# Last three chunk passes: second feed-forward product by seven block products for eight, with a copy of x for the norms

## The chip, the core and the metric

The kernel runs on one core of one Trainium2 chip (trn2). The core's engines have queues of their own: PE (matrix products, with PEld for loading the stationary operand), DVE (elementwise work and reductions), ACT (scaled copies, exponentials, SiLU), POOL (here: memsets and the starting of some DMAs) and SP (here: it only starts DMAs). The instructions of one engine run in the order in which they were written for it, and wait for other engines by semaphores. The metric is device time in microseconds (us).

## The reference

Two layers over 2048 tokens of width 576, each made of a sliding attention and a feed-forward part. In float32:

```
x = x + attention(layernorm(x), wqkv) @ wo
x = x + silu(layernorm(x) @ w1) @ w2          # w1: 576 x 4608, w2: 4608 x 576
x = x + attention(layernorm(x), wqkv) @ wo    # the same weights again
x = x + silu(layernorm(x) @ w1) @ w2
```

Attention has 32 heads of 18 columns; every token looks at itself and at the seven tokens 2, 4, ... 14 before it.

## The kernel before

**Passes.** The tokens are worked in chunks of 512 (NJ = 4 tiles of 128). With two layers this makes eight passes, s = 0 to 7; passes 4 to 7 are the second layer. `front(s)` holds the attention of pass s (norm, query-key-value product in four column units u, attention arithmetic, output projection, norm for the feed-forward part), and `ffn` or `ffn_pairs` its feed-forward part. The attention of pass s+1 runs beside the feed-forward part of pass s.

**Numbers.** Every float32 operand of a product is held as two float16 halves, high and low, and a product takes three float16 products (high by high, high by low, low by high).

**Feed-forward from pass 2 on (`ffn_pairs`).** The 36 row blocks of w1 and w2 are taken as 18 pairs, six groups (g) of three pairs. The first product of a pair is already done by seven block products P1 to P7 for eight (line 1096, 7 matmuls each, from weight forms that were made ahead and lie in DRAM as `wfs`). ACT copies partial results out of PSUM (L1100), DVE adds others (L1103), ACT applies SiLU (L1119, L1121, L1123), ACT makes the high half (L1126) and DVE the low half (L1129, one instruction over 1024 columns). The second product (`second`, L1151) takes 48 matmuls of 128x288 for a pair: 4 token tiles x 2 row blocks x 3 half products x 2 column halves. After each token tile of a group DVE adds the PSUM sum to x (`add_to`, L861). So the second product of a group stands behind the first products of its three pairs, and PE fills the time with first products of the next group. Two PSUM areas (`acc`) take turns for the second product, four banks (z, misc) for the first.

**Attention on DVE.** For one column unit: two products q by k over 2304 columns (L782) with a reduction each (L786), the softmax pieces, four products of weights by v over 1152 columns (L815), and two trees of additions (L822, L823). POOL starts the four small copies between partitions for the halo (L763). The query-key-value product is L682, the projection L854.

**Order.** All work is recorded as operations with an engine, an estimated length, what they read and write, and a priority (`prio`, mostly s plus a fraction; smaller goes first). `Plan.order` plays a list schedule over these estimates and writes the instructions in the order in which they start in it. Buffers are areas of SBUF that several names share; an operation waits until a slot of its name is free.

Of the kernel before, what the change touches and what calls it, by code (L numbers as in the profile page):

```python
# [264 lines left out]
def sliding_attention_silu_ffn(ctx: ExitStack, tc: tile.TileContext, x, wqkv, wo, w1, w2, out):  # L265
# [10 lines left out]


# [50 lines left out]
    part("yb", XA, 1, [8, KH], F32, turns=False)  # L328
# [15 lines left out]
    parts("yf", [(YH, 0), (YO, 0)], [2, KB], F16)  # L344
# [6 lines left out]
    part("w2", W2A, W2N, [2, D], F16)  # L351
# [20 lines left out]
    wfs = [tc.dram_tile([P, 7 * KB], F16, name=f"wfs{q}") for q in range(NP)]  # L372
    wqs = [tc.dram_tile([P, 30 * UC], F16, name=f"wqs{u}") for u in range(NU)]
# [42 lines left out]
    dz = accw[:, NP:NP + NP // 2, :].rearrange("p a b -> p (a b)")  # L416
    pace = cp.tile([1, 1], F32, name="pace")
# [57 lines left out]
    highs = []  # L475
    turned = []
# [21 lines left out]
    def layer_norm(xs, prio, into, on_act, on_pe=False, late=[]):  # L498
# [77 lines left out]
    def raw_wq(u):  # L576
# [3 lines left out]
        raw = lambda k: fl(T(rs[k]).bitcast(F32))[:, :QR]  # L580
# [132 lines left out]
    def attention(s, xT, wq, more=None):  # L713
# [4 lines left out]
        for u in range(NU):  # L718
            kv, qt = Buf("kv"), Buf("qt")
            own = [(kv, j) for j in range(NJ)]  # L720
            if wq is None:
# [8 lines left out]
            else:  # L730
                w = wq(u)
                if blk == 0:
# [3 lines left out]
                    op("POOL", 1.86, clear, [], [(kv, "edge")], pr_)  # L736
                else:
# [5 lines left out]
                    op("SP", 0.8, edge, [("eds", lay, par, u)], [(kv, "edge")], pr_, nbytes=20000, lanes=2)  # L743
                for j in range(NJ):
# [31 lines left out]
            keys = own + [(kv, "halo"), (kv, "edge")]  # L776
            lg, pe, mx, sm = Buf("lg"), Buf("pe"), Buf("mx"), Buf("mx")
            for j in range(0, NJ, 2):
# [9 lines left out]
                op("DVE", 2.49, mul, keys + [(qt, j), (qt, j + 1)], [pr], pr_)  # L788
                op("DVE", 2.49, red, [pr], [(lg, j)], pr_)
# [8 lines left out]
            def soft_b(pe=pe, sm=sm):  # L798
# [5 lines left out]
            op("DVE", 1.42 if blk == 0 else 0.98, soft_a, [], lgs + [mx], pr_)  # L804
            op("ACT", 0.36, lambda pe=pe, lg=lg: nc.scalar.activation(T(pe), T(lg), AF.Exp, scale=DH ** -0.5),
               lgs, [pe], pr_ - 0.2, table="exp")
            op("DVE", 1.38, soft_b, [], [pe, sm], pr_)
            for j in range(0, NJ, 2):
                pr = Buf("pr")

                for a in range(2):
# [5 lines left out]
                    op("DVE", 1.28, mul, keys + [pe], [(pr, a)], pr_, after=formed[-1:])  # L817
# [6 lines left out]
                op("DVE", 2.55, tree, [], [(pr, 0), (pr, 1), (o, j, u), (o, j + 1, u)], pr_, after=formed[-1:])  # L824
                if s == 0:
                    marks.append(op("POOL", 1.3, lambda j=j, u=u: nc.gpsimd.tensor_copy(
                        pace, T(o)[0:1, j, u * UC:u * UC + 1]), [(o, j, u)], ["pace"], -5))
# [69 lines left out]
    def raw_split(f0, prio):  # L897
# [440 lines left out]
```

## Time and profile before

| what | value |
|---|---|
| three timed runs | 2138.58, 2142.57, 2148.47 us (median 2142.57) |
| span of the profiled execution, first to last instruction | 2139.6 us |
| busy, whole span | PE 2114.5, DVE 1640.1, ACT 977.0, POOL 365.9 us |
| read from DRAM, written | 307.32 MB, 67.68 MB |
| DMA engines, mean rate | 199 GB/s |

The profile records no total of its own for the profiled execution beside the span; the span lies 1.0 us above the fastest of the timed runs and 3.0 us under their median. Busy time of PE counts each matmul from start to a modelled end, and neighbouring matmuls overlap, so the rate of PE is read from starts, not from the mean length of one.

### The profile page before, as it was taken

To read this page: it belongs to the slowest core of one execution; us is meant where nothing else is said; L and a number is where in the kernel's file an instruction comes from. 1 tells how busy PE (TensorE), PEld (TensorE's weight loads), DVE (VectorE), ACT (ScalarE), POOL (GpSimd) and SP (SyncE) were. 2 spreads that over 40 slices of the span, in tenths; PEclk is the share of its full clock that TensorE was granted. 3 is DMA by queue.
4 is the path that set the end of the run, shared out by engine and by line. 5 is a ranking of instruction groups with operands and counts; after the bars stand their busy time and mean duration, and the time that the engine had idled before them with its cause. 6 is when DMAs were issued, how large, how long until landed. Compare 5 with 4: busy or idle time off the path is not lost.

```text
span 2139.6 us, 41351 instructions
## 1 busy us (share of the span) xinstructions
PE 2114.5 (99%) x16233; PEld 1576.2 (74%) x16233; DVE 1640.1 (77%) x2599; ACT 977.0 (46%) x1803; POOL 365.9 (17%) x585
## 2 busy tenths in 40 slices
PE   8999899999999999999999999999999999999999
PEld 5556466656667888877788777887788877888887
DVE  8999999999977997548975599746997569853322
ACT  7555787644254553344424344343443434333332
POOL 2223656234242430001100010000000000000000
PEclk9999999999999999999999999999999999999999
DMA  6576777677799987775748765596565965566551
GB/s 182 154 228 245 250 262 247 197 266 237 197 234 287 325 248 209 175 214 167 211 121 224 201 180 160 138 248 190 157 175 146 250 178 165 162 156 199 152 169 62
DMA packets 334235, 426.21 MB, mean 199 GB/s; under 512 B 145608, under 2 KB 262708, under 8 KB 330072
## 3 DMA queue, kind: packets, MB, share of 16 engines
q1 hardware_dynamic: 293720, 293.19, 49.5%
q0 software_dynamic: 38304, 129.28, 18.8%
q8 instruction: 127, 2.08, 0.4%
q10 hardware_dynamic: 2016, 1.11, 0.2%
q14 instruction: 68, 0.56, 0.1%
HBM read 307.32 MB, written 67.68 MB: 175 GB/s over the span
## 4 chain that ended last, share of the span: by engine, by line
PE 88%; DMA 6%; DVE 3%; issue 1%; ACT 1%; SPq 1%; POOL 0%; ACTq 0%; DVEq 0%; POOLq 0%
PE acc L1151 28%; PE z L1096 13%; PE misc L1096 13%; PE z L1193 9%; PE acc L1212 9%; PE z L682 7%; PE acc L854 5%; PE misc L682 5%; DMA w<-wfs 1%; DMA xb<-yo 1%; DMA h<-in_A_wqkv_dram 1%; DMA w<-in_B_w_dram 1%; DMA w<-w2s 1%; DMA yo<-yh 0%; DMA x<-xd 0%
## 5 line engine op out<-in xcount | busy, mean ns | idle before, releaser
L1151 PE MATMUL acc<-w,h 128*128 128x288 f16 x5184 | 669.0, 286 | 1.6 <-DVE x L861 1.0
L1151 PEld LDWEIGHTS <-h 128*128 128x128 f16 x5184 | 507.2, 98 | 126.8 <-issue 2.2
L1096 PEld LDWEIGHTS <-w 128*128 128x128 f16 x5292 | 517.3, 98 | 72.0 <-DMA w<-wfs 3.7
L1096 PE MATMUL z<-xb,w 128*128 128x256 f16 x2653 | 335.5, 273 | 2.3 <-DMA w<-wfs 1.7
L1096 PE MATMUL misc<-xb,w 128*128 128x256 f16 x2639 | 335.7, 273 | 1.1 <-DVE hs L1103 0.9
L861 DVE SCALAR_TENSOR_TENSOR x<-acc,d,x 128x576 f32<-128x576 f32 x183 | 148.5, 812 | 129.8 <-PE acc L1151 122.2
L1212 PE MATMUL acc<-w,h 128*128 128x288 f16 x1728 | 215.4, 286 | 0.0
L682 PEld LDWEIGHTS <-xa 128*128 128x128 f16 x1344 | 131.0, 98 | 112.9 <-issue 2.1
L1212 PEld LDWEIGHTS <-h 128*128 128x128 f16 x1728 | 168.4, 98 | 44.2
L782 DVE TENSOR_TENSOR prs<-qt,kvs 128x2304 f32<-128x2304 f32 x64 | 163.4, 2552 | 10.3 <-DMA kvs<-kvs 9.4
L815 DVE TENSOR_TENSOR prs<-kvs,pe 128x1152 f32<-128x1152 f32 x128 | 170.8, 1351 | 0.5
L786 DVE TENSOR_REDUCE lg<-prs 128x128 f32<-128x2304 f32 x64 | 163.0, 2547 | 1.0
L822 DVE TENSOR_TENSOR prs<-prs 128x1152 f32<-128x1152 f32 (+1 forms) x128 | 135.1, 1055 | 3.1
L1129 DVE SCALAR_TENSOR_TENSOR h<-wq,sh,h 128x1024 f16<-128x1024 f32 x60 | 76.8, 1280 | 73.3 <-ACT h L1126 73.3
L1193 PE MATMUL z<-xb,w 128*128 128x512 f16 x588 | 129.1, 379 | 3.3 <-ACT w L931 1.6
L682 PE MATMUL z<-wq,xa 128*128 128x432 f16 x658 | 124.4, 346 | 0.0
L854 PE MATMUL acc<-wo,yo 128*128 128x288 f16 x896 | 114.2, 286 | 3.7 <-DMA yo<-yh 2.0
L1100 ACT ACTIVATE wq<-z 128x256 f32<-128x256 f32 x94 | 35.6, 381 | 171.4 <-PE z L1096 171.4
L1193 PEld LDWEIGHTS <-w 128*128 128x128 f16 x588 | 57.3, 98 | 72.0 <-DVE w L933 2.9
L854 PEld LDWEIGHTS <-yo 128*128 128x128 f16 x896 | 87.3, 98 | 27.9 <-DMA yo<-yh 2.8
L763 POOL DMA_DIRECT2D kvs<-kvs x64 | 34.0, 538 | 419.1 <-ACT qt L751 418.9
L682 PE MATMUL misc<-wq,xa 128*128 128x432 f16 x518 | 99.1, 346 | 2.7 <-ACT xa L463 1.3
(229 smaller groups left out, 2578.7 us busy)
## 6 DMA issues: line engine op xcount, KB each, us to landing
w<-wfs SPq DMA_DIRECT2D x756, 160.0 KB, 3.4
w<-w2s SPq DMA_DIRECT2D x252, 288.0 KB, 4.4
wq<-wqs SPq DMA_DIRECT2D x17, 1080.0 KB, 6.2
kvs<-kd POOLq DMA_DIRECT2D x8, 1584.0 KB, 9.2
w<-w1s SPq DMA_DIRECT2D x36, 320.0 KB, 4.3
wfs<-xa POOLq DMA_DIRECT2D x18, 640.0 KB, 4.9
w2s<-w POOLq DMA_DIRECT2D x36, 288.0 KB, 4.1
w1s<-wq POOLq DMA_DIRECT2D x30, 320.0 KB, 4.0
```

Source lines behind the costliest of these rows:

```text
L682: nc.tensor.matmul(T(m)[:, :3 * UC], a, b, start=n == 0, stop=n == len(pl) - 1)
L782: nc.vector.tensor_tensor(T(pr), T(qt)[:, j:j + 2, None, :].to_broadcast([P, 2, W, UC]), win(T(kv), j, 2), op=ALU.mult)
L786: nc.vector.tensor_reduce(T(lg)[:, j:j + 2].rearrange("p a w h -> p (a w h)"), T(pr).rearrange("p a w (h d) -> p (a w h) d", d=DH), axis=A ...
L815: nc.vector.tensor_tensor(T(pr)[:, a].rearrange("p w (h d) -> p w h d", d=DH), v, T(pe)[:, j + a, :, :, None].to_broadcast([P, W, UH, DH]) ...
L822: nc.vector.tensor_tensor(t[:, :, 0:h, :], t[:, :, 0:h, :], t[:, :, h:2 * h, :], op=ALU.add)
L854: nc.tensor.matmul(T(acc)[:, h, 0:288], a, b[:, h * 288:(h + 1) * 288], start=n == 0, stop=n == len(pl) - 1)
L861: nc.vector.scalar_tensor_tensor(t, T(acc)[:, :, 0:288], d, t, op0=ALU.mult, op1=ALU.add)
L1096: nc.tensor.matmul(t, w[:, u, :], v[:, r, :], start=first and m == 0, stop=m == 6, skip_group_check=True)
L1129: op("DVE", 1.2, lambda hq=hq, h=h, sc=sc: nc.vector.scalar_tensor_tensor(T(h)[:, 1].rearrange("p f t -> p (f t)"), T(hq).rearrange("p r t ...
L1151: nc.tensor.matmul(T(acc)[:, h, 0:288], T(hb[t])[:, a, f, j * P:(j + 1) * P], T(wbs[t][f])[:, w, h * 288:(h + 1) * 288], start=t == 0 and ...
L1193: nc.tensor.matmul(T(z), v, u, start=m == 0, stop=m == len(pl) - 1)
L1212: nc.tensor.matmul(T(acc)[:, h, 0:288], T(hb[q])[:, a, j * P:(j + 1) * P], T(wbs[q][0])[:, w, h * 288:(h + 1) * 288], start=q == 0 and m = ...
```

## The change

In passes 5, 6 and 7 the second product is done in blocks too (`ffn_twice`, `seconds`): tokens in two halves, columns in two halves, the two row blocks of a pair as the third dimension; seven block products (`SECOND`) take the place of eight. Each is 18 matmuls of 128x288 for a group of three pairs. For this the activations of a pair are kept as seven rows of 256 tokens in place of four: POOL makes four of them by subtractions and one addition (L1268), the high and low halves are made in two pieces (rows 0 to 2 over 768 columns, rows 3 to 6 over 1024; L1273 on ACT, L1276 on DVE). A group has seven additions to x (L1316) in place of four.

Of the seven weight blocks three are column halves of w2 as stored (the store order becomes column half, then high and low), and four are sums. `prepare_second` makes these once per pair and stores them as `wts`: pairs 0 to 8 after the attention arithmetic of pass 4, pairs 9 to 17 after that of pass 5. It uses the area of the key-value buffers, so the query-key-value products of units 0 and 1 of passes 5 and 6 wait for the last store of these forms (`hold`).

In the second layer the norm ahead of the attention reads a copy of x that is loaded a second time, into the area of the attention products (`xp` in `prs`), after the attention arithmetic of the pass before. x itself lies in tiles of two token blocks. Priorities: DVE work of the attention of passes 6 and 7 gets a later one (`pd`, with LEAD), and the second products of a pass's last group get pp + SEAM. Some estimated lengths change. Pass 7 has buffers of its own for more slots (`q2e`, `wte`).

```diff
+S3 = 5
+LEAD = 0.05
+SEAM = 1.0
...
+    part("xp", PR, 1, [NJ, D], F32)
...
-    part("w2", W2A, W2N, [2, D], F16)
+    part("w2", W2A, W2N, [2, 2, KH], F16)
...
+    parts("h2", [(HA, 0), (HA, FB), (HA, 2 * FB), (W2A, 0), (W2A, FB)], [2, 7, 2 * P], F16)
+    parts("q2", [(WQA, 20 * 3 * UC), (W2A, 2 * FB)], [7, 2 * P], F32)
+    parts("wt", [(HA, 3 * FB + i * WB) for i in range(4)] + [(W2A, 3 * FB + i * WB) for i in range(3)]
+          + [(WQA, 20 * 3 * UC + FB)], [2, KH], F16)
+    parts("q2e", [(WQA, 0), (WQA, 20 * 3 * UC), (W2A, 2 * FB)], [7, 2 * P], F32)
+    parts("wte", [(t, i * WB) for t in (PR, O, XA) for i in range(8)], [2, KH], F16)
+    parts("v2", [(KV, 0), (KV, 10 * WB)], [20 * KH], F16)
...
+                hold = {S3: [("wts", NP // 2 - 1)], S3 + 1: [("wts", NP - 1)]}.get(s, []) if u < 2 else []
...
+            pd = pr_ if s <= S3 else pr_ - 0.5 + 0.1 * u + LEAD
...
+    def prepare_second(q, prio, after):
...
+        def sums():
+            t = rows6()
+            for r, x, y in ((3, 1, 0), (1, 5, 1), (4, 5, 3), (2, 2, 4)):
+                nc.gpsimd.tensor_tensor(t[:, r], t[:, x], t[:, y], op=ALU.subtract)
+        op("POOL", 3.4, sums, [(b, 0)], [(b, 0)], prio)
+        op("ACT", 1.2, lambda: nc.scalar.activation(split()[:, :, 0, :], rows6()[:, 1:5], AF.Copy, scale=wst[:, q:q + 1]),
+           [(b, 0), "wsc"], [(b, 1)], prio)
+        op("DVE", 1.4, lambda: nc.vector.scalar_tensor_tensor(split()[:, :, 1, :], rows6()[:, 1:5], wst[:, q:q + 1], split()[:, :, 0, :],
+                                                              op0=ALU.mult, op1=ALU.subtract), [(b, 0), (b, 1)], [(b, 1)], prio)
+        op("POOL", 0.57, lambda: nc.gpsimd.dma_start(wts[q], T(b)[:, 12 * KH:]), [(b, 1)], [("wts", q)], prio, nbytes=P * 4 * KH * 4)
...
+    SECOND = (1, 5, 6, 3, 7, 2, 4)
+    def ffn_twice(s, xf, xs):
...
+                for r, u, v, o in ((4, 6, 3, ALU.add), (5, 4, 0, ALU.subtract), (2, 1, 5, ALU.subtract), (6, 0, 6, ALU.subtract)):
+                    op("POOL", 0.75, lambda hq=hq, r=r, u=u, v=v, o=o: nc.gpsimd.tensor_tensor(T(hq)[:, r], T(hq)[:, u], T(hq)[:, v], op=o),
+                       [(hq, u), (hq, v)], [(hq, r)], pd - 0.01)
+                for r0, r1, sh in ((0, 3, shx), (3, 7, shy)):
...
+    def seconds(s, g, q0, n, hb, xs):
...
+        wb = {(k, t): load_wt(q0 + t, k, s - 0.5, "wt" if s < NL * NC - 1 else "wte") for k in SECOND for t in range(n)}
+        for i, k in enumerate(SECOND):
...
+                        for j in js:
+                            for t in ts:
+                                for m, (a, w) in enumerate(((0, 0), (0, 1), (1, 0))):
+                                    nc.tensor.matmul(T(acc)[:, j, 0:KH], T(hb[t])[:, a, row[k], j * P:(j + 1) * P], T(wb[k, t])[:, w, :],
...
-            o = attention(s, layer_norm(X[s], s - 1.0, "xa", False, late=[("wfs", NP - 1, 1)]), lambda u: load_wq(u, s - 1.0, "wz"))
+            o = attention(s, layer_norm(load_x(s, s - 1.0, attended[-1:], into="xp"), s - 1.0, "xa", False, late=[("wfs", NP - 1, 1)]), lambda u: load_wq(u, s - 1.0, "wz"))
...
-        (ffn if s < S2 else ffn_pairs)(s, XT[s], X[s])
+        (ffn if s < S2 else ffn_pairs if s < S3 else ffn_twice)(s, XT[s], X[s])
...
+        if s in (S3 - 2, S3 - 1):
+            for q in range(*((0, NP // 2), (NP // 2, NP))[s - S3 + 2]):
+                prepare_second(q, s + 0.9, attended[s + 1:s + 2])
```

How the instructions then stand is shown at three places. The first is DVE in the third group of pass 5, between additions to x, where the attention of pass 6 (L815, L822, L823 before; L813, L854 of the changed file, the same operations) runs beside the feed-forward part. Before:

```order
L861 SCALAR_TENSOR_TENSOR x_80<-acc_104,d_270,x_80 128x576
L1129 SCALAR_TENSOR_TENSOR h<-wq,sh_267,h 128x1024
L815 TENSOR_TENSOR prs<-kvs,pe_87 128x1152
L822 TENSOR_TENSOR prs<-prs 128x2x576
L822 TENSOR_TENSOR prs<-prs 128x2x288
L823 TENSOR_TENSOR o<-prs 128x2x144
L861 SCALAR_TENSOR_TENSOR x_81<-acc_105,d_270,x_81 128x576
```

And of the change, at the same group (L1316 is the addition to x, L1244 an addition of a first product, L1276 one half of the low halves):

```order
L854 TENSOR_TENSOR o<-prs 128x2x144
L1316 SCALAR_TENSOR_TENSOR x_76<-acc_99,d2x,x_76 128x2x288
L1244 TENSOR_TENSOR wq<-z_95,wq 128x256
L1244 TENSOR_TENSOR wq<-misc_96,wq 128x256
L1276 SCALAR_TENSOR_TENSOR w_87<-w_87,shx 128x768
L1316 SCALAR_TENSOR_TENSOR x_75<-acc_98,d2x,x_75 128x2x288
L1276 SCALAR_TENSOR_TENSOR w_87<-w_87,shy 128x1024
L813 TENSOR_TENSOR prs<-qts,kvs 128x2304
```

The additions to x stand closer together (seven to a group), and the low halves are two instructions, so more feed-forward work lies between two pieces of attention.

The second place is POOL beside the feed-forward part of pass 6, near its last halo copies. Before, POOL starts the four halo copies of a unit and then DMAs of x to the output, and nothing else:

```order
L763 DMA kvs<-kvs 112x1152
L763 DMA kvs<-kvs 15x1152
L763 DMA kvs<-kvs 112x864
L763 DMA kvs<-kvs 14x864
L1234 DMA out_dram<-x_78 128x576
```

With the change (L1268 is the arithmetic on the activations, L793 the halo):

```order
L1268 TENSOR_TENSOR wq<-wq 128x256 x4
L1268 TENSOR_TENSOR w_87<-w_87 128x256 x3
L793 DMA kvs<-kvs 112x1152
L793 DMA kvs<-kvs 15x1152
L793 DMA kvs<-kvs 112x864
L793 DMA kvs<-kvs 14x864
L1268 TENSOR_TENSOR w_87<-w_87 128x256
```

Four instructions of arithmetic for every pair stand in POOL's queue between the halo copies, and here a pair's last one stands behind a halo.

The third place is ACT in pass 7, one pair. Before (L1100 copies out of PSUM, L1121, L1123 and L1119 are SiLU, L1126 the high half; the last row is the next pair's):

```order
L1100 ACTIVATE wq<-z_100 128x256
L1100 ACTIVATE wq<-z_101 128x256 x2
L1121 ACTIVATE wq<-wq,accw 128x512
L1123 ACTIVATE wq<-wq,accw 128x256
L1119 ACTIVATE wq<-z_101,accw 128x256
L1126 ACTIVATE h<-wq,sh_267 128x1024
L1100 ACTIVATE wq<-misc_103 128x256
```

With the change (L1241 copies out of PSUM, L1262, L1264 and L1260 are SiLU, the two L1273 the high halves; tiles `w_87` are this pair's, `wq` the next one's):

```order
L1241 ACTIVATE w_87<-z_94 128x256
L1241 ACTIVATE w_87<-misc_96 128x256 x2
L1262 ACTIVATE w_87<-w_87,accw 128x2x256
L1264 ACTIVATE w_87<-w_87,accw 128x256
L1260 ACTIVATE w_87<-misc_96,accw 128x256
L1241 ACTIVATE wq<-z_95 128x256
L1273 ACTIVATE h<-w_87,shy 128x1024
L1273 ACTIVATE h<-w_87,shx 128x768
L1241 ACTIVATE wq<-misc_97 128x256
```

Between SiLU and the high halves now lies POOL's arithmetic, and a copy out of PSUM for the next pair stands behind the high halves on ACT.

More of the change, by code (lines that the diff above doesn't have):

```diff
@@ L372, in sliding_attention_silu_ffn @@
     wfs = [tc.dram_tile([P, 7 * KB], F16, name=f"wfs{q}") for q in range(NP)]
+    wts = [tc.dram_tile([P, 4 * 2 * KH], F16, name=f"wts{q}") for q in range(NP)]
     wqs = [tc.dram_tile([P, 30 * UC], F16, name=f"wqs{u}") for u in range(NU)]
@@ L534, in layer_norm @@
                 prio = -19
-            y, yh = Buf("y"), Buf("yh")
+            own = xs[j][0].tag == "xp"
+            y, yh = xs[j] if own else Buf("y"), Buf("yq" if own else "yh")
             def norm(j=j, y=y):
@@ L720, in attention @@
             own = [(kv, j) for j in range(NJ)]
+            free = formed[-1:] if u == 1 and s > NC else ()
             if wq is None:
@@ L735, in clear @@
                         nc.gpsimd.memset(T(kv)[0:1, 3:7], 0.0)
-                    op("POOL", 1.86, clear, [], [(kv, "edge")], pr_)
+                    op("POOL", 1.86, clear, hold, [(kv, "edge")], pr_, after=free)
                 else:
@@ L753, in attention @@
                         op("PE", 2.56 * (b - a) / 14, lambda j=j, m=m, w=w, a=a, b=b: qkv_matmul(xT, w, j, m, a, b),
-                           [(xT, j)] + [w.keys[5 * h + k] for k in range(a // 3, (b + 2) // 3) for h in range(2)],
-                           [m, (kv, "hold")] if lay else [m], pr_)
+                           [(xT, j)] + hold + [w.keys[5 * h + k] for k in range(a // 3, (b + 2) // 3) for h in range(2)],
+                           [m, (kv, "hold")] if lay else [m], pr_, after=free)
                     op("ACT", 0.78, evac, [m, ("su", u)], [(kv, j), (qt, j)], pr_ - (0 if s else 9))
@@ L823, in tree @@
                     nc.vector.tensor_tensor(T(o)[:, j:j + 2, u * UC:(u + 1) * UC], t[:, :, 0, :], t[:, :, 1, :], op=ALU.add)
-                op("DVE", 2.55, tree, [], [(pr, 0), (pr, 1), (o, j, u), (o, j + 1, u)], pr_, after=formed[-1:])
+                done = op("DVE", 2.55, tree, [], [(pr, 0), (pr, 1), (o, j, u), (o, j + 1, u)], pd, after=formed[-1:])
                 if s == 0:
@@ L827, in attention @@
                         pace, T(o)[0:1, j, u * UC:u * UC + 1]), [(o, j, u)], ["pace"], -5))
+        attended.append(done)
         return o
@@ L832, in project @@
         pr_ = s - 1.0
+        pd = pr_ if s <= S3 else pr_ - 0.5 + 0.4 + LEAD
         for j in range(NJ):
@@ L1031, in sliding_attention_silu_ffn, with forms @@
     P_ORDER = ("P5", "P1", "P3", "P6", "P2", "P7", "P4")
-    def forms(xs, prio, home="yb", late=[]):
+    def forms(xs, prio, home="yb"):
         st, mv, nt = Buf("st"), Buf("mv"), Buf("nt")
@@ L1242, in write_x, with load_x @@
                     op("SP", 0.5, lambda j=j, c0=c0: nc.sync.dma_start(x_rows(out, c, j)[:, c0], T(xs[j])[:, c0]),
-                       [(xs[j], h)], [], pd, nbytes=P * D * 2)
-    def load_x(s, prio, ahead=None):
-        lay, c = divmod(s, NC)
-        xs = [Buf("x") for _ in range(NJ)]
+                       [(*xs[j], h)], [], pd, nbytes=P * D * 2)
+        if s == NL * NC - 1 and S3 < NL * NC:
+            for th, ch in ((0, 1), (0, 0), (1, 1), (1, 0)):
+                for i in range(2):
+                    j, c0 = 2 * th + i, slice(ch * KH, (ch + 1) * KH)
+                    op("SP", 0.38, lambda j=j, c0=c0: nc.sync.dma_start(x_rows(out, c, j)[:, c0], T(xs[j])[:, c0]),
+                       [(*xs[j], ch)], [], pd, nbytes=P * D * 2)
+    def load_x(s, prio, ahead=None, into=None):
+        lay, c = divmod(s, NC)
+        if into is None:
+            halves = [Buf("x") for _ in range(2)]
+            xs = [(halves[j // 2], j % 2) for j in range(NJ)]
+        else:
+            b = Buf(into)
+            xs = [(b, j) for j in range(NJ)]
         for j in range(NJ):
             src = (lambda j=j: x_rows(x, c, j)) if lay == 0 else (lambda j=j: xd[c][j])
-            if ahead:
+            if ahead and lay == 0:
                 op("POOL", 0.54, lambda j=j, src=src: nc.gpsimd.dma_start(T(xs[j]), src()), [], [xs[j]], prio,
```

221 lines of the change are left out of this document (171 added, 50 removed).

## The prediction

> **What bounds the kernel now.** I read the page first: its span, the busy shares and the 40 slices.
>
> ```profile
> span 2139.6 us, 41351 instructions
> ...
> PE 2114.5 (99%) x16233; PEld 1576.2 (74%) x16233; DVE 1640.1 (77%) x2599; ACT 977.0 (46%) x1803; POOL 365.9 (17%) x585
> ...
> PE   8999899999999999999999999999999999999999
> ...
> DVE  8999999999977997548975599746997569853322
> ...
> POOL 2223656234242430001100010000000000000000
> ```
>
> PE is busy in every slice, POOL nearly idle in the second half, and DVE reaches 9 in places there. Busy matmuls overlap, so I checked the rate of PE in order of time, in the first full group of pass 7, and two pieces of the chain that ended last, of the attention (start us, length us):
>
> ```profile
> 1957.50 6.04 PE L1151 MATMUL acc<-w,h 128*128 128x288 f16 x48
> 1963.38 0.93 PE L1096 MATMUL z<-xb,w 128*128 128x256 f16 x7
> 1964.15 0.93 PE L1096 MATMUL misc<-xb,w 128*128 128x256 f16 x7
> ```
>
> ```profile
> 1485.15 5.11 PE misc L682 x28
> ...
> 1614.82 3.43 PE acc L854 x28
> ```
>
> 48 matmuls of 128x288 take from 1957.50 to 1963.38, that is 0.1225 us each; seven of 128x256 take 0.765 us, 0.1093 each; L682 takes 5.11/28 = 0.1825, L854 0.1225. A group of pass 7 has 147 and 144 matmuls of the first two kinds: 16.07 + 17.64 = 33.71 us. The table by stage has it at 33.69, and shows the stretches that hold most of passes 5 and 6 (columns: length, then busy time of PE, PEld, DVE, ACT, POOL, clock, DMA share, GB/s):
>
> ```profile
> 1957.67:1991.36 33.69, 33.69 (x293) 28.49 (x292) 10.58 (x16) 11.79 (x21) 0.00 (x0) 1.00 0.52 156
> ```
>
> ```profile
> 450.00:700.00 250.00, 248.03 (x1666) 162.70 (x1664) 221.15 (x314) 112.11 (x175) 83.61 (x123) 1.00 0.89 257
> ...
> 1410.00:1660.00 250.00, 249.88 (x2024) 197.91 (x2023) 186.98 (x290) 97.33 (x191) 10.70 (x20) 1.00 0.67 185
> 1660.00:1910.00 250.00, 250.00 (x2021) 197.50 (x2020) 187.46 (x290) 97.40 (x194) 10.69 (x20) 1.00 0.65 180
> ```
>
> So passes 5 to 7 are PE's own work with no gap, at full granted clock; a matmul removed there is time saved, as long as nobody else becomes late. DVE has 63 us to spare in 250.
>
> **What the change removes.** For each pair 48 matmuls of the second product become 42. Three passes of 18 pairs: 54 x 6 = 324 matmuls fewer; 324 x 0.1225 = **39.7 us**. Each still loads its own stationary operand, as before.
>
> **What it adds on DVE.** The rows by form, of the last 730 us:
>
> ```profile
> L861 DVE SCALAR_TENSOR_TENSOR x<-acc,d,x 128x576 f32<-128x576 f32 x74 | 60.3, 814 | 87.5 <-PE acc L1151 87.4
> L1129 DVE SCALAR_TENSOR_TENSOR h<-wq,sh,h 128x1024 f16<-128x1024 f32 x36 | 46.1, 1281 | 58.5 <-ACT h L1126 58.5
> L815 DVE TENSOR_TENSOR prs<-kvs,pe 128x1152 f32<-128x1152 f32 x32 | 42.8, 1351 | 0.1
> L782 DVE TENSOR_TENSOR prs<-qt,kvs 128x2304 f32<-128x2304 f32 x16 | 40.9, 2556 | 6.2 <-DMA kvs<-kvs 5.8
> L786 DVE TENSOR_REDUCE lg<-prs 128x128 f32<-128x2304 f32 x16 | 40.8, 2551 | 0.4
> L1103 DVE TENSOR_TENSOR wq<-z,wq 128x256 f32<-128x256 f32 x58 | 23.8, 419 | 25.8 <-ACT wq L1100 20.4 <-PE z L1096 5.3
> ...
> L822 DVE TENSOR_TENSOR prs<-prs 128x1152 f32<-128x1152 f32 x16 | 21.6, 1352 | 0.2
> ...
> L822 DVE TENSOR_TENSOR prs<-prs 128x576 f32<-128x576 f32 x16 | 12.1, 758 | 0.6
> L823 DVE TENSOR_TENSOR o<-prs 128x288 f32<-128x288 f32 x16 | 7.3, 458 | 0.6
> ```
>
> The split of 768 columns is new; between the 576 columns of L861 (0.81) and the 1024 of L1129 (1.28) I take 1.0. A pass then has 18 x 1.0 more for the splits and 18 more additions to x at 0.81 (42 for 24), 33 us together: 187 + 33 = 220 of the some 240 us that passes 5 and 6 keep. That fits as an average, but not everywhere. The attention of pass 6 cannot begin until the weight forms are stored, so it is pressed into a part of pass 5. I counted the order of the change there, from the first block product of the second group to the third of the fifth, 23 block products, on both queues. PE: 476 of 128x256, 414 + 112 of 128x288, 112 of L682: 52.0 + 50.7 + 13.7 + 20.4 = 137 us. DVE, 213 instructions: attention arithmetic 81 us (6 of L782, 6 of L786, 16 of L815, 8 trees at 2.57, softmax 8), splits of nine pairs 20.6, 28 additions of first products 11.8, 23 additions to x 18.7, norms and projection about 27: 159 us by mean lengths. Instructions that do not use the one before start earlier:
>
> ```profile
> 1583.28 0.42 DVE L1103 TENSOR_TENSOR hs<-z,hs 128x256 f32<-128x256 f32 x1
> 1583.62 0.41 DVE L1103 TENSOR_TENSOR hs<-misc,hs 128x256 f32<-128x256 f32 x1
> ```
>
> 0.34 us apart at a length of 0.42; with 0.08 off for some 90 of the 213, DVE needs 152. That is 15 more than PE's 137, and PE cannot run away from it: the block product after the next needs the PSUM area that DVE's addition empties. An addition may lag by one block product (18 x 0.1225 = 2.2 us) and a little more, so 12 to 15 are lost; I take **12**, and 0 to 15 as bounds, 0 if work between is overlapped better than counted. The same count over the first four groups of pass 6 gives PE 161, DVE 151: 10 us of slack. In pass 7 DVE has no attention beside it and waits.
>
> **What it adds on POOL.** Four instructions of 256 columns for a pair, reading two tiles in SBUF. The trace has no such instruction. Nearest rows:
>
> ```profile
> L734 POOL MEMSET kvs<- 2x864 f32 x12 | 9.7, 810 | 120.7 <-DVE prs L815 120.7
> ...
> masks.py:199 POOL TENSOR_SCALAR_AFFINE_SELECT ident<-ident 128x128 f16<-128x128 f16 x1 | 0.3, 289 | 0.1
> ```
>
> Between 0.29 (half the columns) and 0.81 (over three times as many, none read); I take 0.6, twice the first. A chain of four is then 2.4 us in a pair's 10.5. POOL has room. But one kind of POOL instruction in the trace reads SBUF, a copy of a single element, and its length depends on DVE:
>
> ```profile
> 82.53 2.56 POOL L826 COPY pace<-o 1x1 f32<-1x1 f32 x1 [1.44 <-DVE o L823]
> ...
> 132.90 0.18 POOL L826 COPY pace<-o 1x1 f32<-1x1 f32 x1 [17.84 <-DVE o L823]
> ```
>
> ```profile
> 82.48 2.56 DVE L782 TENSOR_TENSOR prs<-qt,kvs 128x2304 f32<-128x2304 f32 x1
> ...
> 132.96 1.55 DVE L668 SCALAR_TENSOR_TENSOR wo<-w,su,wo 128x576 f16<-128x576 f32 x2 [0.19 <-ACT wo L665]
> ```
>
> Begun 0.05 us after an L782 of DVE, which reads two tiles, it ends with that, 2.56 us later; with DVE idle at its start it takes 0.18. So POOL's arithmetic will wait for DVE. Whether DVE also waits for POOL the trace cannot show, since a one-element copy is over at once. Bounds for DVE's wait per POOL instruction: 0, and 0.6, its whole length. I take 0.2, a third, because only part of DVE's instructions read two tiles in SBUF, and some begin when POOL is nearly done. In the overfull stretch of pass 5 are nine pairs, 36 such instructions: **8 us**. In pass 6, 48 x 0.2 = 10 meets the slack of 10: 0. [...]
>
> **What I cost at nothing.** The weight forms: on POOL, ACT and DVE a few us for each of 18 pairs, in groups around the change of pass, where by the same count DVE has 24 to 28 us of work beside 54 to 56 of PE; the queue of PE holds the query-key-value product behind the last of them, and if that is late, PE waits: at most some 6 us, twice. ACT: two high halves for one, 17 us more a pass on 97 busy in 250. DMA, all on SP's queue: seven loads of 144 KB a pair for two of 288, and x again, some 9 MB a pass, 185 to about 227 GB/s. The window 450 to 700 above ran 257 GB/s with PE busy 248 of 250, so that is the cover.
>
> ```profile
> w<-wfs SPq DMA_DIRECT2D x756, 160.0 KB, 3.4
> w<-w2s SPq DMA_DIRECT2D x252, 288.0 KB, 4.4
> ```
>
> Passes 5 and 6 hold eight block weights, and a block product uses three in 2.2 us, so a freed place has about 3.7 us when products stand back to back, and a landing takes 3.4 to 4.4. First products mostly stand between; without them it costs up to 1 us each, some 20 in all.
>
> **The sum.** 2139.6 - 39.7 + 12 + 8 = 2119.9 for the profiled execution. Its span lies 3.0 under the median of the runs, so I say **2123 us** against 2142.57, 0.9% faster. Likeliest case, 2114 to 2132: 0.45.
>
> **Rivals.**
> - *Everything is hidden*: DVE's excess is taken up by lag and POOL does not hold DVE. 2142.6 - 39.7 = 2103, up to 2114. For it: no DVE instruction in the trace was held; against: the count of 152 to 137. Chance 0.18.
> - *POOL and DVE shut each other out*, slower. If each POOL instruction keeps DVE for its 0.6 us, pass 5 loses 12 + 36 x 0.6 = 34, pass 6 48 x 0.6 - 10 = 19, and the later halves make ACT and PE wait besides: 2142.6 - 39.7 + 53 = 2156 and more, up to 2175. It is even with the gain at 39.7 = 12 + 84t - 10, t = 0.45 us. [...] Chance 0.15.
> - *Gain given back in small waits*: port 0.3 to 0.45 us, block weights late by 5 to 15, forms late by 5. 2132 to 2153. Chance 0.22.
> - *The change does not do what it says*: the order has 324 matmuls fewer on PE, in the passes named. I leave nothing for it.
>
> **How the numbers follow.** The range goes from the bottom, 2103, to 2153; it leaves out the slow rival at 0.15 and a little below. A measurement of this kernel can tell about 0.5%, 10.7 us, from no change: faster is under 2132 (0.45 + 0.18), same 2132 to 2153 (0.22), slower above (0.15).
>
> **What would show it.** Groups of pass 7 at 147 x 0.1093 + 126 x 0.1225 = 31.5 us: the 39.7 is right. PE waits of 15 to 25 us between the second and the fifth group of pass 5, released by DVE, and hardly any in pass 6: my terms. [...] PE waiting for ACT L1273 or for block weights in passes 6 and 7 would make me wrong, as would a wait at the start of the query-key-value product of pass 5 or 6.

## The result, and the profile after

The changed kernel takes 2192.41 us, median of four runs (2187.96 to 2198.82), beside 2140.57 us for the kernel before (2137.69 to 2148.47): ratio 1.0239, interval 1.0217 to 1.0261. It is 2.4% slower; 2123, a little faster, was forecast. The profiled execution has a span of 2186.2 us, 46.6 more than before.

The page of the change, parts 1 and 2 (busy time of each engine; the span in 40 slices):

```profile
span 2186.2 us, 42078 instructions
...
PE 2096.9 (96%) x15909; PEld 1548.1 (71%) x15909; DVE 1794.8 (82%) x2729; ACT 1038.2 (47%) x1875; POOL 645.2 (30%) x891
...
PE   8999899999999999999999999989889899998999
...
DVE  8999999999978999699943799856999699974454
...
POOL 2223665233233230110222111352332234222222
```

PE has 324 matmuls fewer, and for the first time slices under 9 in the second half. DVE stands at 9 in longer stretches, POOL has work to the end. Two windows of 250 us, which were full before, and two groups of pass 7 (columns as in the prediction: length, busy time of PE, PEld, DVE, ACT, POOL, clock, DMA share, GB/s):

```profile
1410.00:1660.00 250.00, 222.26 (x1709) 168.69 (x1707) 201.40 (x242) 106.33 (x195) 92.12 (x96) 0.97 0.73 204
1660.00:1910.00 250.00, 230.04 (x1814) 177.16 (x1812) 221.16 (x309) 106.27 (x201) 81.45 (x84) 0.99 0.74 203
2043.80:2077.50 33.70, 33.70 (x296) 28.67 (x294) 16.36 (x25) 15.12 (x27) 8.55 (x12) 1.00 0.72 209
2077.50:2106.70 29.20, 29.20 (x254) 24.69 (x253) 14.79 (x22) 12.55 (x21) 8.59 (x12) 1.00 0.73 209
```

In pass 7, with no attention beside it, two groups take 62.9 us, 31.45 each, with PE full: what was forecast there came. The loss lies before that, most of it in passes 5 and 6. Who PE waited for, from 1150 us on (total, times, longest, in us; the six longest of 31 rows):

```profile
PE misc L1237 <- DVE wq L1244: 7.2, 3, 4.8
PE z L1237 <- DMA w<-wfs: 6.6, 4, 4.8
PE z L1237 <- ACT wq L1241: 4.9, 4, 2.0
PE misc L1237 <- DMA xb<-yo: 4.6, 2, 4.1
PE misc L1237 <- ACT wq L1241: 4.2, 3, 2.0
PE z L710 <- DVE wq L1244: 3.9, 1, 3.9
```

No one wait carries it: all rows sum to 27 us for DVE, 19 for DMA and 18 for ACT, 64 together, where the same view of before has 3.0 in three rows. To close the sum I took from the trace the time from the start of each matmul to the start of the next, beside the median of its shape. Matmuls at their medians sum to 2059.22 us (before 2098.75), which is 39.5 less; excess of more than 1.3 medians, a wait, to 98.9 (25.8); smaller excess, slow matmuls, to 22.6 (10.4). So -39.5 + 73.1 + 12.2 = +45.8, of the 46.6 that the span grew. The 85 us of excess that came on top can be placed by this sum of starts, each pass taken from the first matmul of its second product to that of the next pass: pass 5 loses 45 us, pass 6 25 and pass 4, which still has the old product, 19 (before: 0.7, 1.3 and 3.1).

The slow matmuls are the clock: the 12 us that came on top lie in stretches where the granted clock is 0.50. The longest wait of pass 5, in order of time (start, length, and in brackets the idle time ahead with its releaser), and the same stretch in slices of 3 us, where the column behind POOL is the granted clock:

```profile
1547.16 6.29 POOL L1268 TENSOR_TENSOR w<-w 128x256 f32<-128x256 f32 x4 [2.97 <-ACT w L1264]
1547.51 3.56 DVE L846 TENSOR_TENSOR prs<-kvs,pe 128x1152 f32<-128x1152 f32 x2
...
1551.11 2.96 DVE L853 TENSOR_TENSOR prs<-prs 128x1152 f32<-128x1152 f32 x2
...
1554.48 0.42 DVE L1244 TENSOR_TENSOR wq<-misc,wq 128x256 f32<-128x256 f32 x1
1554.81 2.62 DVE L846 TENSOR_TENSOR prs<-kvs,pe 128x1152 f32<-128x1152 f32 x2
1554.95 1.65 PE L1237 MATMUL misc<-xb,w 128*128 128x256 f16 x7 [4.80 <-DVE wq L1244]
1557.46 2.15 DVE L853 TENSOR_TENSOR prs<-prs 128x1152 f32<-128x1152 f32 x2
```

```profile
1551.00:1554.00 3.00, 0.00 (x0) 0.00 (x0) 2.93 (x3) 1.45 (x2) 2.45 (x2) 1.00 1.06 305
1554.00:1557.00 3.00, 1.65 (x7) 1.02 (x7) 2.96 (x5) 0.63 (x1) 0.00 (x0) 0.57 0.58 196
1557.00:1560.00 3.00, 0.00 (x0) 0.00 (x0) 2.90 (x4) 0.00 (x0) 0.00 (x0) 0.50 0.21 58
1560.00:1563.00 3.00, 2.51 (x8) 1.05 (x8) 3.00 (x6) 1.20 (x3) 1.33 (x1) 0.50 0.02 5
1563.00:1566.00 3.00, 3.00 (x17) 1.74 (x16) 2.96 (x2) 1.29 (x4) 2.92 (x2) 0.72 0.00 0
1566.00:1569.00 3.00, 3.00 (x24) 2.12 (x22) 2.48 (x1) 2.33 (x4) 1.86 (x3) 1.00 0.47 129
```

The addition L1244 that empties PE's PSUM area takes 0.42 us but stands behind 7.0 us of attention on DVE, from 1547.51 to 1554.48: two products of 1152 columns and their tree. Beside POOL's four subtractions these pieces take 3.56 and 2.96; the next pair of them, with POOL idle, takes 2.62 and 2.15. PE is idle for 4.80 us, and when it starts again the granted clock is half, 0.50 in the 3 us from 1554.95: seven matmuls take 1.65 us for 0.93.

### The profile page after: what moved, and what is told of

It reads as the page before. It is cut to its first block, busy times and chain, and to the rows that moved or that the text cites. A ratio compares the mean times of both kernels' runs of the same rounds, so it can differ in the third digit from the quotient of the medians.

```text
span 2186.2 us, 42078 instructions
## 1 busy us (share of the span) xinstructions
PE 2096.9 (96%) x15909; PEld 1548.1 (71%) x15909; DVE 1794.8 (82%) x2729; ACT 1038.2 (47%) x1875; POOL 645.2 (30%) x891
## 4 chain that ended last, share of the span: by engine, by line
PE 54%; DVE 13%; DMA 7%; POOL 2%; ACT 2%; issue 2%; SPq 1%; DVEq 0%; ACTq 0%; POOLq 0%
PE acc L1334 12%; PE acc L1307 8%; PE z L1176 6%; PE misc L1176 6%; PE misc L710 4%; PE z L1237 4%; PE misc L1237 4%; PE acc L1395 3%; PE z L1376 3%; PE z L710 3%; PE acc L887 2%; DVE prs L846 1%; DVE prs L853 1%; DMA xb<-yh 1%; DVE x L1316 1%
## 5 line engine op out<-in xcount | busy, mean ns | idle before, releaser
L1334 PE MATMUL acc<-w,h 128*128 128x288 f16 x2592 | 338.4, 286 | 2.5 <-DVE h L1209 1.9
L1237 PEld LDWEIGHTS <-w 128*128 128x128 f16 x2646 | 261.7, 99 | 82.5 <-issue 32.2
L1334 PEld LDWEIGHTS <-h 128*128 128x128 f16 x2592 | 253.5, 98 | 64.4 <-DVE h L1209 2.6
L1176 PEld LDWEIGHTS <-w 128*128 128x128 f16 x2646 | 259.2, 98 | 43.2 <-issue 5.0
L1395 PE MATMUL acc<-w,h 128*128 128x288 f16 x1728 | 215.8, 286 | 2.2 <-DMA w<-w2s 2.2
L1395 PEld LDWEIGHTS <-h 128*128 128x128 f16 x1728 | 168.4, 98 | 46.8 <-issue 2.6
L1237 PE MATMUL misc<-xb,w 128*128 128x256 f16 x1351 | 177.9, 277 | 21.6 <-DVE wq L1244 7.2
L1268 POOL TENSOR_TENSOR wq<-wq 128x256 f32<-128x256 f32 x120 | 111.4, 940 | 204.4 <-ACT wq L1264 178.2
L1176 PE MATMUL misc<-xb,w 128*128 128x256 f16 x1316 | 166.5, 273 | 2.0 <-DMA xb<-yh 1.2
L813 DVE TENSOR_TENSOR prs<-qts,kvs 128x2304 f32<-128x2304 f32 x64 | 163.8, 2559 | 4.7 <-DMA kvs<-kvs 3.9
L1307 PEld LDWEIGHTS <-h 128*128 128x128 f16 x1386 | 135.4, 98 | 40.0 <-issue 4.5
L817 DVE TENSOR_REDUCE lg<-prs 128x128 f32<-128x2304 f32 x64 | 162.9, 2546 | 0.9
L1316 DVE SCALAR_TENSOR_TENSOR x<-acc,d2x,x 128x576 f32<-128x576 f32 (+1 forms) x127 | 102.5, 809 | 70.4 <-PE acc L1307 69.8
L1268 POOL TENSOR_TENSOR w<-w 128x256 f32<-128x256 f32 x96 | 94.6, 998 | 184.5 <-ACT w L1264 170.5
L710 PE MATMUL misc<-wq,xa 128*128 128x432 f16 x644 | 123.1, 346 | 6.3 <-DVE w L1244 1.8
L1088 POOL TENSOR_TENSOR kvs<-kvs 128x288 f32<-128x288 f32 x72 | 65.2, 916 | 190.1 <-DVE yh L474 109.1
```

The source lines that it names most:

```text
L710: nc.tensor.matmul(T(m)[:, :3 * UC], a, b, start=n == 0, stop=n == len(pl) - 1)
L813: nc.vector.tensor_tensor(T(pr), T(qt)[:, j:j + 2, None, :].to_broadcast([P, 2, W, UC]), win(T(kv), j, 2), op=ALU.mult)
L817: nc.vector.tensor_reduce(T(lg)[:, j:j + 2].rearrange("p a w h -> p (a w h)"), T(pr).rearrange("p a w (h d) -> p (a w h) d", d=DH), axis=A ...
L1176: nc.tensor.matmul(t, w[:, u, :], v[:, r, :], start=first and m == 0, stop=m == 6, skip_group_check=True)
L1237: nc.tensor.matmul(t, w[:, u, :], v[:, r, :], start=first and m == 0, stop=m == 6, skip_group_check=True)
L1268: op("POOL", 0.75, lambda hq=hq, r=r, u=u, v=v, o=o: nc.gpsimd.tensor_tensor(T(hq)[:, r], T(hq)[:, u], T(hq)[:, v], op=o), [(hq, u), (hq, ...
```

## Experiments: which passes, and the changes of pass

Three kernels move the first pass with the new product (`S3`); the first has it in none.

```diff
-S3 = 5
+S3 = 8
...
-        if s in (S3 - 2, S3 - 1):
+        if S3 < NL * NC and s in (S3 - 2, S3 - 1):
```

> The new second product is made in no pass (S3 = 8, no weight forms); the own copy of x, the later place of a group's last products, the new areas and the changed order stay. All theories that put the loss into the new product expect the time of before, 2140 within 6 us. Rival: the surroundings cost something themselves, then 2146 to 2155.

> The new product in the last pass only (S3 = 7), where no attention runs beside it; weight forms are made after the attentions of passes 6 and 7. Gain of pass 7: 108 matmuls x 0.1225 = 13.2 us. If the loss comes from attention beside the new product (on DVE and POOL): 2128 to 2134. If the weight forms or the block weights are late by themselves, they cost 5 to 15 us here too: 2135 to 2145.

> The new product in passes 6 and 7. If the pressed attention beside the first pass with the new product is what costs (45 us lost in pass 5 of the change against 13 saved), pass 6 now takes that place: 2155 to 2170. If each pass with attention costs the same, about half of the loss of the change: 2150 to 2160. If pass 5 were special: 2130 to 2140.

Measured: 2159.99 with none (ratio to before 1.0088, 1.0070 to 1.0105), 2153.06 with pass 7 alone, 2187.61 with passes 6 and 7. All three came out above every case that I expected. So the new order alone, with no new product, loses 18.5 us; I had no term for that. It is not a share of the 52 that can be taken off them, since the change waits at other places: in its last group of pass 3 it loses 1 us by the sum of starts, e1_off 7. Pass 7 gives 7 back. Pass 6 costs 34.5, and pass 5 only 5 more. That fits with where the attention lies that must wait for the weight forms: in e3 it lies beside pass 6, which loses 56 us by the sum of starts, where the same pass of the change loses 25 and pass 5 loses 45. The loss goes with the first pass, not with each.

The waits of PE in e1_off from 1150 us on, all but one of 0.6 us, and one change of pass there in order of time:

```profile
PE z L1176 <- DMA xb<-yo: 3.8, 1, 3.8
PE z L1176 <- DMA xb<-yh: 3.8, 2, 3.1
PE misc L1176 <- DMA xb<-yo: 3.5, 1, 3.5
```

```profile
1151.07 3.51 SPq L1151 DMA_TRANSPOSE xb<-yo  x2
...
1155.02 1.63 PE L1334 MATMUL acc<-w,h 128*128 128x288 f16 x12
1160.46 1.65 PE L1176 MATMUL z<-xb,w 128*128 128x256 f16 x7 [3.81 <-DMA xb<-yo]
```

At each of three changes of pass PE waits 3 to 4 us for a transposed norm form of the next pass, and behind the one shown it runs at half clock (0.50 from 1160 to 1166 us, seven matmuls in 1.65 again). Ahead of the wait stand only 12 matmuls of the last group's second product. `SEAM` gives their due time; three kernels put it back:

```diff
-SEAM = 1.0
+SEAM = 0.18
```

> e1_off with SEAM = 0.18, the value that gives the last group's second products the due time that they had before. e1_off waited 3.3 to 4.0 us at each of three changes of pass for the transposed norm forms, and PE's clock was low for some us behind each: about 6 us each, 19 in all. If the later place of the last products is the cause: 2140 to 2145. If it is the other surroundings (forms kept in other areas, single transposes, own copy of x): 2153 to 2162.

> The change with SEAM = 0.18 and nothing else. If the later place costs the same here as in e1_off: 2170 to 2178. If with the new product the later place is what covers the wait for the forms of the next pass, as its waits at a change of pass are no longer than those inside a pass: 2188 to 2205.

> e2_from7 with SEAM = 0.18: if the seam costs what e1_off lost (18) and pass 7 gains 7 to 13: 2128 to 2136, faster than the kernel before. If the seam is not the cause: 2150 to 2155.

Measured: 2151.77 from 2159.99 without the new product, between its two cases, with runs from 2144 to 2165; the profiled one, of span 2142.6, has none of the three waits. But 2209.45 from 2192.41 with it, and 2160.43 from 2153.06 in pass 7 alone, where the runs of both spread by 13 us and more. The due time is thus one cause in e1_off, and a cover in the change, where the order has more to wait for; e6 and e7 came out above both cases that I expected of them. The other side of that order is what it believes: the planner places work by its own estimate of when a transposed form lands. Telling it that the form lands 4 us later, and nothing else:

```diff
-                    queues[e].append([now + dur + self.DMA_IN, o.nbytes / self.DMA_RATE, o])
+                    queues[e].append([now + dur + self.DMA_IN + o.more, o.nbytes / self.DMA_RATE, o])
...
-                   [(f, 0), (f, 1)], [(x, a)], prio, nbytes=P * KB * 4)
+                   [(f, 0), (f, 1)], [(x, a)], prio, nbytes=P * KB * 4, more=4.0)
```

> e1_off (the new product in no pass) with the landing of a transposed form 4 us later in the planner. If the 18 us of e1_off are the order's wrong belief about that landing: 2141 to 2147. If the forms are late for a cause that the order cannot meet: 2155 to 2162.

Measured: 2142.67, ratio 0.9999 (0.9983 to 1.0015). The same place in e18_off_late:

```profile
1151.73 3.22 PE L1177 MATMUL z<-xb,w 128*128 128x256 f16 x28
1154.79 4.57 PE L1335 MATMUL acc<-w,h 128*128 128x288 f16 x36
```

36 matmuls for 12 stand ahead of the product that needs the form, and the wait is gone. With that estimate changed, all 18 us of e1_off are gone. The same cure was not run on the change itself.

The block weights of the second product share SP's queue with those of the first. Two kernels give them a later due time:

```diff
-        wb = {(k, t): load_wt(q0 + t, k, s - 0.5, "wt" ...
+        wb = {(k, t): load_wt(q0 + t, k, s - 0.45, "wt" ...
```

> The change with block weights of the second product given a later due time than those of the first (s - 0.45 for s - 0.5), so that in SP's queue they no longer stand ahead of the first product's. At 1998 the profile of the change has 24 such loads ahead of the ten that PE then waits 4.8 us for, with low clock behind. Theory D (SP's order): this wait goes and some of the other 9 us of waits for DMA: 2175 to 2187. If another wait takes its place: 2188 to 2197.

> e7_from7_seam with the later due time for block weights: e7 waited 8.8 us at the start of pass 7 for the first product's block weights, with 2.8 us of low clock behind. If SP's order is the cause: 2145 to 2150. If they are late for another reason (the DMA engines full at the change of pass): 2157 to 2163.

Measured: 2187.60 from 2192.41 and 2157.55 from 2160.43. e10 lies between its two cases; the wait of 4.8 us is gone from its trace, and by the sum of starts its last group of pass 6 loses 2.6 us for 7.7. e12 lies in the case in which the order on SP is not the cause, and its 3 us are within the spread of its runs (2150 to 2167). So that order is worth some 5 us in the change; in e12 no gain is shown.

## Experiments: inside the passes

Five kernels leave something out. In e4_nopool POOL's instructions L1268 (three subtractions and an addition for a pair, called subtractions below) work on 2 columns:

```diff
-...nc.gpsimd.tensor_tensor(T(hq)[:, r], T(hq)[:, u], T(hq)[:, v], op=o),
+...nc.gpsimd.tensor_tensor(T(hq)[:, r, 0:2], T(hq)[:, u, 0:2], T(hq)[:, v, 0:2], op=o),
```

> The change with POOL's four subtractions cut from 256 to 2 columns each, and the halves made from repeated rows of the same size; the same number of instructions, order and lengths elsewhere (the subtractions are left out of the result). Theory A (POOL's arithmetic: chains of 0.73 us alone, up to 1.8 beside two-input instructions of DVE, DVE held 0.19 us for each, ACT's queue and then PE behind them): 2140 to 2160, of the loss of 52 over before at least 30 goes. Theory B (DVE's own additions and splits, 33 us a pass): 2175 to 2187, DVE gets back only its 27 us of stretch, a third of it on the path.

In e8_shortadd the additions to x work on 8 columns a row (`T(acc)[:, a:b, 0:8]` for `0:KH`):

> The change with each addition of a second product to x cut from 288 to 8 columns a row (most of these sums are left out of the result): 42 additions a pass of some 0.2 us for 0.81, DVE is lighter by some 25 us a pass, POOL does all its arithmetic. Theory B (DVE's own load): of the 52 lost, 25 to 35 come back, 2157 to 2167. Theory A (POOL's chains, DVE held by them): 2175 to 2190.

In e9_noforms `prepare_second` issues nothing, and a block weight is loaded from a stored w2:

```diff
-        op("SP", 0.8, load, ["wsc"], [(b, 0)], prio, nbytes=P * 4 * KH * 4, after=after, lanes=2)
...
+        op("POOL", 0.01, lambda: None, ["wsc"], [("wts", q)], prio, after=after)
```

> The change without the making of weight forms: no load, subtractions, halves and store for the 18 pairs; block weights are loaded from the stored w2 instead (the second product is then of other weights), the same sizes and count. The query-key-value products of passes 6 and 7 no longer wait for a store. Theory C (the forms cost, by their work at the two changes of pass and by pressing the attention of pass 6 into four fifths of pass 5): 10 to 25 us of the loss go, 2167 to 2182. If C is wrong, under 5 us: 2187 to 2195.

Measured: e4 2167.81, 25 us less than the change; e8 2178.20, 14 less; e9 2158.45, 34 less (its seven runs lie from 2149 to 2161). Of A, B and C none is the whole. A came out below its bound of 30, B at half of what it claimed, and C, which I had costed at nothing, is the largest, above the 10 to 25 that I expected. In e4 and e8 the order stays as it is in the change; in e9 it shifts, the attention above all.

How POOL costs is in the trace of the change. L1268 takes 0.73 us where DVE is idle (median), and four of them then 2.9; the mean is 0.94 to 1.00, and beside attention:

```profile
1624.71 6.36 POOL L1268 TENSOR_TENSOR wq<-wq 128x256 f32<-128x256 f32 x4 [12.49 <-ACT wq L1264]
1627.52 2.97 DVE L853 TENSOR_TENSOR prs<-prs 128x1152 f32<-128x1152 f32 x2
1629.90 0.94 ACT L1273 ACTIVATE h<-wq,shx 128x768 f16<-128x768 f32 x1 [5.27 <-POOL wq L1268]
1630.52 0.86 DVE L854 TENSOR_TENSOR o<-prs 128x288 f32<-128x288 f32 x1
```

L854, 0.46 us alone, takes 0.86. Summed over all forms of DVE in passes 5 and 6, those that meet a subtraction are together some 31 us longer than at the length of their form without one: 31/144 = 0.22 us for each subtraction. So both take longer beside each other. L1316, L1244 and L817, which read one SBUF tile, alone or with PSUM, keep their length (0.81, 0.42 and 2.55 us alone, 0.81, 0.41 and 2.54 at the median beside a subtraction); but L874, which reads one as well, took 1.00 us at 1645 us beside a subtraction, for 0.51 alone. And ACT stands in line behind POOL:

```profile
1598.36 6.49 POOL L1268 TENSOR_TENSOR wq<-wq 128x256 f32<-128x256 f32 x4 [9.48 <-ACT wq L1264]
...
1604.19 0.94 ACT L1273 ACTIVATE h<-wq,shx 128x768 f16<-128x768 f32 x1 [3.20 <-POOL wq L1268]
...
1606.07 0.36 ACT L1241 ACTIVATE w<-z 128x256 f32<-128x256 f32 x1
...
1606.49 1.69 PE L1237 MATMUL z<-xb,w 128*128 128x256 f16 x14 [2.75 <-ACT w L1241]
```

The copy L1241 that frees PE's area takes 0.36 us; it waits behind two high halves that wait for a chain of POOL of 6.49.

The weight forms could cost by their work or by the wait they put on the query-key-value products of passes 5 and 6 (the expectations of e9 and e13 name passes 6 and 7; `hold` stands in 5 and 6, which run beside the feed-forward parts of passes 4 and 5). e13_pressed keeps the wait and leaves out the work:

```diff
-        op("POOL", 0.01, lambda: None, ["wsc"], [("wts", q)], prio, after=after)
+        op("HOLD", 16.0, lambda: None, ["wsc"], [("wts", q)], prio, after=after)
```

> e9_noforms, with the query-key-value products of passes 6 and 7 held in the order to the place that they have in the change, by nine steps of 16 us on no engine: no instruction is added. If the forms cost because the attention is pressed into a part of the pass: 2180 to 2192, as the change. If their work on POOL, ACT, DVE and the queues costs: 2155 to 2165, as e9_noforms (2158).

Measured: 2185.09. The first such product of pass 6 in the change, in e9_noforms, in e13_pressed and in the kernel before:

```profile
1478.46 2.72 PE L710 MATMUL misc<-wq,xa 128*128 128x432 f16 x14
```

```profile
1401.58 2.72 PE L710 MATMUL misc<-wq,xa 128*128 128x432 f16 x14
```

```profile
1468.63 2.72 PE L710 MATMUL z<-wq,xa 128*128 128x432 f16 x14
```

```profile
1460.60 2.72 PE L682 MATMUL misc<-wq,xa 128*128 128x432 f16 x14
```

Begun 77 us later in the change than in e9 (67 in e13), the attention lies beside fewer groups of pass 5, and that is 27 of the 34 us by the times; 7 are left for the work of the forms. The sum of starts agrees on the first: pass 5 loses 45 us in the change, 18 in e9 and 46 in e13. On the work it says more: pass 4 loses 19, 5 and 5, so the work costs some 14 us there, of which e13 hides a part because its pass 6 loses 35 us for 25 and 25, for a cause that stays open. And the kernel before begins this product at 1460.60, only 18 us ahead of the change: the 27 us are the price against an attention that the new order could begin 59 us earlier than the kernel before did, not against that kernel. Why the forms take so long, one of the change in order of time:

```profile
1113.30 0.57 SPq L1082 DMA_DIRECT2D kvs<-in_B_w_dram  x1
1117.43 3.29 POOL L1088 TENSOR_TENSOR kvs<-kvs 128x288 f32<-128x288 f32 x4 [10.79 <-DMA kvs<-in_B_w_dram]
1122.92 1.24 ACT L1090 ACTIVATE kvs<-kvs,accw 128x1152 f16<-128x1152 f32 x1
1124.25 1.41 DVE L1092 SCALAR_TENSOR_TENSOR kvs<-kvs,accw 128x1152 f16<-128x1152 f32 x1
1125.96 0.58 POOL L1094 DMA_DIRECT2D wts<-kvs  x1 [5.24 <-DVE kvs L1092]
1132.00 0.55 SPq L1082 DMA_DIRECT2D kvs<-in_B_w_dram  x1
```

Six us of arithmetic, but 18.7 from load to load: one place at a time, each freed by the store. Last, all three left out:

> e9_noforms, e4_nopool and e8_shortadd together: no weight forms, POOL's subtractions on 2 columns, additions to x on 8. If these three are the whole loss inside the passes and their prices add: 2192 - 34 - 25 - 14 = 2119; full gain would be 2101 to 2104. If they are three ways to relieve the same stretch, they add up to less: 2130 to 2150.

Measured: 2138.39, ratio to before 0.9975 (0.9964 to 0.9986). The three give 54 together, not the 73 of their sum; so they relieve in part the same stretches. Three windows of it: the second to fourth group of pass 5, then the change to pass 6 and that to pass 7:

```profile
1526.20:1634.20 108.00, 106.88 (x919) 89.46 (x917) 91.07 (x177) 43.58 (x74) 13.70 (x36) 1.00 0.81 220
1675.20:1727.20 52.00, 46.13 (x346) 33.85 (x344) 34.17 (x41) 20.45 (x37) 9.55 (x20) 0.97 0.83 256
1885.50:1965.40 79.90, 69.78 (x570) 56.34 (x568) 36.11 (x86) 36.02 (x81) 7.99 (x30) 0.94 0.90 239
```

Inside the pass PE is full but for 1 us in 108. What is missing to full gain, by the median of before in the same session 2138.4 - (2143.1 - 39.7) = 35.0, lies at the changes of pass, where PE waits for DMAs (norm forms, `wqs`, `wfs`) and the clock falls: by the sum of starts 37 us of this kernel's excess lie in the groups at its four changes from pass 3 to pass 7. No run here removes them. One more kernel puts the attention on DVE back behind the feed-forward work (`LEAD = 0.55`):

> The change with LEAD = 0.55, which puts the attention on DVE back behind the feed-forward work of its pass, as before the change. If the waits in pass 5 come from additions standing behind pieces of attention of 2.6 to 6.6 us on DVE (4.8 and 3.9 us at 1550 to 1560): the waits inside the passes shrink, but the attention ends late and the change of pass waits: 2185 to 2200 in sum, moved and not removed. If only the order on DVE is wrong and it has time in sum: 2165 to 2180.

Measured: 2204.64, 12 more than the change, a little above the case that the wait is moved and not removed. The sum of starts shows the move: the second to fifth group of pass 5 lose 11 us for 32, but the last group of pass 5 loses 33 for 11, and that of pass 6 28 for 8. This other place for the attention on DVE gains nothing over the whole pass; it only moves the wait.

## Experiments: versions

> The change with the four subtractions for a pair's weight forms on DVE (about 1.7 us) for POOL (3.7 us by the profile). One place is left in the area for most forms, and they follow each other some 18 us apart, so a chain shorter by 2 us lets nine of them end 10 to 18 us earlier. If the length of the chain sets when the attention may begin: 2178 to 2188. If DVE has no room for 31 us more, or the chain is set by its DMAs: 2190 to 2200.

> The new product in the last pass alone, subtractions for the forms on DVE, block weights loaded after the first product's, SEAM = 1.0. e2_from7 had 2153, of which 18 are waits at the changes of pass that e1_off has too; a shorter chain and SP's order give back 3 to 10: 2143 to 2150, still no faster than before. If the forms' chain is not on the path here: 2150 to 2156.

> e16_from7_dve, with the planner told that a transposed norm form lands 2 us later than it assumed; only the order changes. e16 waited 3.8 and 4.0 us for such forms at two changes of pass, with 5.4 us of low clock behind: if more work is put ahead of the products that need them, 2133 to 2141, a little faster than the kernel before. If the order moves the wait to another place: 2144 to 2155.

```diff
-                nc.gpsimd.tensor_tensor(t[:, r], t[:, x], t[:, y], op=ALU.subtract)
-        op("POOL", 3.4, sums, [(b, 0)], [(b, 0)], prio)
+                nc.vector.tensor_tensor(t[:, r], t[:, x], t[:, y], op=ALU.subtract)
+        op("DVE", 1.7, sums, [(b, 0)], [(b, 0)], prio)
```

The diff is that of e15; e16 has `S3 = 7` and e10's due time besides, e17 `more=2.0` besides that. Measured: e15 2186.31, in its first case and a little better than the change. But the attention of pass 6 begins only 7 us earlier (1471.8 for 1478.5), and by the sum of starts the gain lies in pass 4 (12 us lost for 19), with 45 in pass 5 as before, so it does not show that the chain's length was what counts in pass 5. e16 2147.54, ratio 1.0028 (1.0011 to 1.0045); e17 2150.03, ratio 1.0033 (1.0020 to 1.0046). e17 lost the waits at the earlier changes of pass, but has one of 5.1 us and others for norm forms at the change to pass 7: its second case, the wait moved. No version with the whole computation beat the kernel before.

## Why the prediction was wrong

- **324 matmuls, 39.7 us**: right. PE's own work fell by 39.5 us, groups of pass 7 take 31.45 us for the 31.5 foretold.
- **DVE 12 and POOL's hold 8, in the second to fifth group of pass 5**: place and engine right, size too small. The waits released by DVE there sum to 17 us, within the 15 to 25 foretold, but the four groups lose 32 us by the sum of starts: ACT ends another 5 us of waits, DMAs 2, and half clock comes on top. The hold came out at 0.22 us for the 0.2, which had been a guess of a third, so that is luck (its reason, that only instructions with two SBUF tiles are held, was an estimate, and L874 above, with one, was longer too); a subtraction takes 0.73 for 0.6. (36 x 0.2 is 7.2, too, and not 8.) What the step left out is that DVE's share does not have to be exceeded for PE to wait: a short addition waits behind 7 us of attention, a short copy on ACT behind POOL's chain of 6.5, and each of the five idle stretches of 3 us and more (3.02 to 4.80) is followed by half clock, 0.50 in the next 3 us (slow matmuls cost 12 us more in all).
- **Pass 6 at 0**: wrong. It lost 25 us: 11 in the four groups for which I had counted 10 of slack, 14 in its last two groups, at the change to pass 7.
- **"What I cost at nothing"**: the step that failed most. The sum put 20 us against the gain, and the excess grew by 85. Beside the 32 above, 32 of them lie at the changes of pass (the last group of passes 4 and 5, the last two of pass 6), 10 in the first four groups of pass 6 and 8 in the first five of pass 4; for none of these places had the sum a term. The weight forms stood beside it with waits of at most 6 us, twice. Without them 34 us go: 27 because the attention begins earlier, the rest their work. I had seen that the attention is pressed, but priced it by sums of busy time over 23 block products. At the changes of pass the new order, with `SEAM` and an earlier attention, runs PE into norm forms and weights that have not landed: 18.5 us even without the new product (e1_off), some 35 in e14_all3. What would remove these waits in the change stays open.
- **The slower rival**, POOL and DVE shutting each other out, named an effect that is there, with the wrong price: each takes longer beside the other (L854 0.86 us for 0.46, L1268 0.94 to 1.00 in the mean for 0.73), but that costs DVE some 0.22 us for a subtraction and not 0.6, and 25 us in all with the chains (e4). No run shows a port, by which the rival of small waits calls its 0.3 to 0.45 us; what the runs show in its place are these 0.22. Below its break-even of 0.45 it should have left a gain; most of the loss came at places to which no rival gave more than a few us, and so the range, up to 2153, missed by 39 us.

## What to carry to other kernels

Where an engine is full in every slice, a saving on it can be lost wherever an order written from estimates lets it wait: look at each place where it hands over to others (here the changes of pass) and ask how many us of its work the order puts ahead of what must land. Price a step that delays a long stage by the work that the stage then lies beside, not by the step's own busy time. And count a wait of 3 us on TensorE at more than its length where the clock falls behind it, as it did here: behind each of the change's five waits of 3.02 to 4.80 us the granted clock was 0.50 for 3 us.

## What the runs showed of the hardware

A wait of 2.75 us (at 1603 us of the change, shown above) left the matmuls behind it at full clock (1.00 in the next 3 us); after one of 3.02 us seven matmuls took 1.65 us for 0.93, at 0.50:

```profile
1639.76 1.65 PE L1237 MATMUL misc<-xb,w 128*128 128x256 f16 x7 [3.02 <-DVE w L1244]
```

A shorter wait can do the same. One of 2.04 us, close behind two of 0.82 and 1.12, left a granted clock of 0.50 from 1449 to 1452 us, and 14 matmuls took 3.14 us for the 1.69 above:

```profile
1449.00 3.14 PE L1237 MATMUL misc<-xb,w 128*128 128x256 f16 x14 [2.04 <-ACT wq L1241]
```

With full clock behind 2.75 us and half clock behind 2.04, the length of a wait alone does not tell by this trace whether half clock follows. A subtraction on POOL takes 0.195 us at the median over 2 columns (e4_nopool) and 0.73 over 256, so its length does not go with the columns alone.
